# Four engines load the last branch's flag ahead of the experts' stage, and get a branch hint with it

## Chip, cores, metric

The kernel runs on one core of one Trainium2 chip. The metric is the time of one execution in microseconds of device time; the kernel before and the kernel after are compared by their medians over several runs.

## What is computed

The reference is an attention block followed by a mixture of experts. The attention works in chunks of 32 queries, which see 16 keys to the left, 8 to the right and 8 memory keys; its output, with the heads put side by side, is `x` (3072 tokens of 512). Each token goes to the one expert with the largest logit, through two layers, and is weighted by its gate:

```python
for c in range(S // 32):                     # q, k, v: (4, 8, 768, 64)
    a = softmax(scale * q_c @ concat(mem_k, k_ctx).T)
    out[:, :, c_start:c_end] = a @ concat(mem_v, v_ctx)
x = out.transpose(0, 2, 1, 3).reshape(3072, 512)
logits = x @ w_gate                          # 8 experts
e = argmax(logits); gate_w = softmax(logits)[e]
y = gate_w * (maximum(x @ w1[e], 0) @ w2[e]) # w1: (8, 512, 1024), w2: (8, 1024, 512)
```

## The kernel before

There are two programs in the kernel. `ordinary` is the one that these inputs run: it holds for inputs in which no expert gets more than 640 tokens and no sum of exponentials overflows. `general` computes the same for any input. `ordinary` finds out itself whether it was allowed to run, in a flag `good` (L934, a 1x1 tile in SBUF: 1 if its result stands). After it comes `with tc.If(rv == 0)` (L1579), where `rv` is `good` read into a register of each engine (L1137, `values_load`). With these inputs `rv` is 1, so every engine jumps over the code of `general`, which is some hundred instructions on each engine, and the kernel ends.

`ordinary` has two stages.

The **attention stage** (until about 190 us) goes over 32 blocks of 96 queries in a hand-written order (`tc.manual_schedule`): transposes of q and k, scores, exponentials, values, and, a few blocks behind, the routing. Tokens are scattered by expert to `x_dram` in DRAM (L801). Toward its end TensorE already computes up to 256 rows of expert 0 (`do_early`, L1014 writes their `y` on ACT), POOL gathers the rest of expert 0's rows (`xe`, L880), DVE makes sums of weights (`first_sums`, L943), and `count_up` writes `good`. Then the registers are read: `index` (which of 24 code arms each expert takes, TensorE only, L1136) and `rv` (L1137).

The **experts' stage** (from about 190 us to the end) is one `tile_critical` region (L1544) with semaphores of its own. A planner (`op`) has recorded each step with what it reads and writes, and `emit` writes them out with their waits. For each of the 8 experts TensorE enters, by a `Switch` on `index[e]`, one of 24 copies of the same matmuls that differ only in how many tokens they take (L1553). Such a jump goes far, so TensorE gets a hint ahead of it: `switch_hint` names the coming jump and the register that decides it (L1138 for the first expert, L1542 for the others, three steps ahead of an arm's end), and each arm begins with a hint for the jump at its own end. ACT, DVE, POOL and SP run straight on: ACT and DVE take sums out of PSUM and form sums of operands, POOL gathers the next expert's rows (L1293) and sends results to `out` by indirect DMA (L1276, `put`), SP loads weights (L1321). Results go out over five semaphores, `put0` to `put4`. 

On the way into the region every engine waits for all counters of the stage before, so that it is a barrier (L1606: a chain of waits with up to two counters each, and a branch). SP's counter is the last of them, since SP first waits for all work itself. On the way out SP waits until every engine has left the region, and then each engine does the branch at L1579. Behind it, `landed` lets SP wait for the five `put` semaphores, that is, until all output is in DRAM; then all engines meet in a barrier, POOL clears the semaphores, and they meet again (L1606).

## Time and profile before

| | us |
|---|---|
| median of 3 runs | 535.52 (534.76 to 537.1) |
| profiled execution | 532.34 |
| its span, first to last instruction | 530.6 |
| experts' stage, TensorE's first transpose | 190.46 |
| last matmul issued / last store's DMA issued by POOL | 520.8 / 523.9 |
| PE busy | 507.7 (96%) |
| DVE, ACT, POOL busy | 300.0, 245.7, 156.0 |
| granted TensorE clock | 0.994 |

The span's last part is not busy time of any engine: register, branch, wait and semaphore instructions are not counted as busy. They are in the trace all the same, with the engine's name and a q (SPq is SP's sequencer), by line: engine, operation, how many, shortest, median and longest duration in ns, and the start of the first and last in us.

### The profile page before, as it was taken

What the parts mean: (1) busy time and instruction counts of PE and PEld (TensorE: products, weight loads), DVE (VectorE), ACT (ScalarE), POOL (GpSimd) and SP (SyncE); (2) the same over time, 40 slices, a digit from 0 to 9 for tenths busy, and PEclk for the clock granted to TensorE, in tenths of its full rate; (3) what the DMA queues carried; (4) which work ended last, traced back from release to release, by engine and by line L of the source; (5) the groups of instructions that cost most, each with busy time, mean ns of one, the idle gap of its engine ahead of it and who ended that gap; (6) DMA issues with size and microseconds to landing.
All of it is one profiled execution on the core that took longest, in us unless ns stands there. A gap on an engine that the chain in (4) does not pass through costs nothing.

```text
span 530.6 us, 9604 instructions
## 1 busy us (share of the span) xinstructions
PE 507.7 (96%) x3666; PEld 475.7 (90%) x3666; DVE 300.0 (57%) x565; ACT 245.7 (46%) x445; POOL 156.0 (29%) x186
## 2 busy tenths in 40 slices
PE   3999999999999989999999999999999999999992
PEld 3899999999998569999999999977779999999991
DVE  3455656566555246878656557443625767864611
ACT  2466656556632136374553454344216637454311
POOL 2000131323373604354135054121312434412003
PEclk9999999999999999999999999999999999999997
DMA  9999999989982302446406335330505334200002
GB/s 171 154 171 181 182 224 200 224 201 344 303 308 73 88 15 81 172 172 229 176 15 221 96 128 208 102 134 30 195 18 199 139 125 182 81 15 13 1 1 84
DMA packets 81350, 75.02 MB, mean 141 GB/s; under 512 B 39543, under 2 KB 64375, under 8 KB 81281
## 3 DMA queue, kind: packets, MB, share of 16 engines
q1 hardware_dynamic: 71840, 54.60, 41.6%
q0 software_dynamic: 8768, 19.29, 11.0%
q8 instruction: 46, 0.75, 0.6%
q10 hardware_dynamic: 672, 0.18, 0.1%
q14 instruction: 24, 0.19, 0.1%
HBM read 66.13 MB, written 17.50 MB: 158 GB/s over the span
## 4 chain that ended last, share of the span: by engine, by line
PE 83%; issue 9%; DMA 3%; POOL 2%; ACT 1%; DVE 1%; POOLq 0%; ACTq 0%
PE sum_p L511 20%; PE sum_r L511 13%; PE sum_q L511 13%; PE o L511 11%; PE sc L511 8%; PE tqk L516 4%; PE sum_x L516 3%; PE ph L511 3%; PE py L511 3%; PE sum_q L516 2%; PE tx L516 2%; POOL out_dram L1276 2%; DMA xe<-x_dram,rows 1%; DMA x_dram<-xr,dest 1%; DMA kn<-in_k_dram 1%
## 5 line engine op out<-in xcount | busy, mean ns | idle before, releaser
L1276 POOL DMA_INDIRECT out_dram<-y,xe x42 | 51.0, 1214 | 177.1 <-PE sum_q L511 59.9
L1293 POOL DMA_INDIRECT xe<-x_dram,rows x35 | 50.7, 1448 | 49.8 <-PE sum_r L511 29.2
L676 ACT ACTIVATE ex<-sc,cst 128x256 f32<-128x256 f32 x96 | 38.5, 472 | 56.5 <-PE sc L511 56.5
L511 PE MATMUL o<-v,ex 128*96 128x65 f32 x512 | 54.5, 251 | 0.0
L1227 ACT COPY sum_r<-sum_p 128x640 f32<-128x640 f32 x48 | 32.5, 677 | 47.3 <-PE sum_p L511 47.2
L511 PE MATMUL sc<-qT,kT 128*128 128x192 f32 x256 | 50.6, 343 | 1.1 <-ACT qT L627 1.1
L511 PEld LDWEIGHTS o<-v,ex 128*96 128x96 f32 x512 | 49.4, 167 | 0.0
L511 PE MATMUL sum_p<-xsT,w 128*128 128x136 f32 (+6 forms) x256 | 47.6, 329 | 0.5
L511 PE MATMUL sum_r<-t,w 128*128 128x136 f32 (+6 forms) x256 | 45.8, 326 | 0.0
L511 PE MATMUL sum_p<-t,s 128*128 128x136 f32 (+6 forms) x256 | 45.6, 326 | 0.0
L801 POOL DMA_INDIRECT x_dram<-xr,dest x32 | 30.2, 944 | 52.5 <-PE tqk L516 21.3
L511 PE MATMUL sum_q<-t,s 128*128 128x136 f32 (+6 forms) x256 | 45.1, 324 | 0.0
L511 PEld LDWEIGHTS sc<-qT,kT 128*128 128x128 f32 x256 | 43.2, 199 | 1.4 <-issue 1.4
L511 PEld LDWEIGHTS sum_p<-xsT,w 128*128 128x128 f32 x256 | 39.7, 190 | 4.8 <-issue 2.1
L511 PE MATMUL sum_p<-h,w 128*128 128x136 f32 (+6 forms) x256 | 43.8, 324 | 0.0
L511 PEld LDWEIGHTS sum_p<-t,s 128*128 128x128 f32 x256 | 39.7, 190 | 2.6
L511 PEld LDWEIGHTS sum_r<-t,w 128*128 128x128 f32 x256 | 39.6, 190 | 2.6
L511 PEld LDWEIGHTS sum_q<-t,s 128*128 128x128 f32 x256 | 39.8, 190 | 2.3
L511 PEld LDWEIGHTS sum_p<-h,w 128*128 128x128 f32 x256 | 39.5, 190 | 2.3
L1224 DVE TENSOR_TENSOR h<-sum_p,kept 128x640 f32<-128x640 f32 x16 | 13.2, 824 | 48.4 <-ACT sum_r L1227 48.4
L645 DVE COPY kT<-tqk 64x384 f32<-64x384 f32 x62 | 34.3, 554 | 10.4 <-PE tqk L516 9.8
L690 DVE RECIPROCAL inv_all<-o 96x4 f32<-96x4 f32 x64 | 11.4, 179 | 48.0 <-PE o L511 47.7
(154 smaller groups left out, 916.9 us busy)
## 6 DMA issues: line engine op xcount, KB each, us to landing
w<-in_moe_w_dram SPq DMA_DIRECT2D x14, 2048.0 KB, 8.6
kn<-in_k_dram SPq DMA_DIRECT2D x16, 384.0 KB
qn<-in_q_dram SPq DMA_DIRECT2D x16, 384.0 KB
w<-in_moe_w_dram SPq DMA_DIRECT2D x8, 512.0 KB
v<-in_v_dram SPq DMA_DIRECT2D x24, 128.0 KB
v<-in_v_dram SPq DMA_DIRECT2D x24, 112.0 KB
v<-in_v_dram SPq DMA_DIRECT2D x8, 144.0 KB
v<-in_v_dram SPq DMA_DIRECT2D x8, 96.0 KB
```

The lines of the kernel that those rows point to most:

```text
L511: i = nc.tensor.matmul(*args, **more)
L516: i = nc.tensor.transpose(*args)
L645: i = copy(to, of[:, :, 0:PAIRS].rearrange("d a (y z p) -> d a y z p", y=2, z=2))
L676: nc.scalar.activation(ex4[:, :, :, sl], sc4[:, :, :, sl], AF.Exp, bias=mask[:, 3 * x + g : 3 * x + g + 1], scale=D**-0.5)
L690: nc.vector.reciprocal(inv, o[:, :, D])
L801: i = nc.gpsimd.indirect_dma_start(out=x_dram, out_offset=bass.IndirectOffsetOnAxis(ap=dest[:, t : t + 1], axis=0), in_=xr[:, t % NXR].bit ...
L1224: op(eng, one_op(lambda: engines[eng].tensor_tensor(out, a, b, op=how)), reads, writes)
L1227: op("ACT", one_op(lambda: nc.scalar.copy(to, of)), reads, writes)
L1276: return nc.gpsimd.indirect_dma_start(out=out, out_offset=bass.IndirectOffsetOnAxis(ap=which.bitcast(I32), axis=0), in_=y, in_offset=None, ...
L1293: return nc.gpsimd.indirect_dma_start(out=x[:, g].bitcast(I32), out_offset=None, in_=x_dram, in_offset=bass.IndirectOffsetOnAxis(ap=rows[: ...
```

## The change

Two lines are put ahead of the experts' stage. Four engines (POOL, ACT, DVE, SP; not TensorE) compute 1 − rv in a register and run a hint that names the branch of `If` at the kernel's end, which gets a label for that. To compute it they have to have `rv`, so that the load of `good`, which the scheduler puts where a register is first used, stands ahead of the stage on all of them.

```diff
         nc.switch_hint(engines=[nc.tensor], index=[index[e]], n=len(ARMS), label=f"expert{e}")
 
+    for eng in (nc.gpsimd, nc.scalar, nc.vector, nc.sync):
+        tc.mark_branch_hint_location("general", hint=1 - rv, engines=[eng.engine])
     with tc.tile_critical(no_gpsimd_drain=True):
         for e in range(E + 1):
             for s in plan:
@@ -1576,7 +1578,7 @@
             for sem, n in stores:
                 nc.sync.wait_ge(sem, n)
 
-    with tc.If(rv == 0):
+    with tc.If(rv == 0, label="general"):
         landed()
         general(tc, *args)
     landed()
```

In the built program this gives, on each of the four engines, one register operation (`RegisterAlu`) and one `BranchPrefetchHint`. ACT and SP had their load of `good` at that place before; on DVE and POOL it moves there from behind the region. The two moved loads count up the counters of DVE's and POOL's sequencer, which join the counters that every engine waits for on the way into the region: its chain of waits grows by one instruction on each engine, and the counters are paired anew.

## The prediction

> **What bounds the kernel now.** I read the page's head and slices first, then a table of stages, then the sequencer rows of the lines that the change touches (the branch at L1579, the loads of `good` at L1137, the stage's entry and end at L1606 and L1544), and last the DMA view of the tail.

> ```profile
> PE 507.7 (96%) x3666; PEld 475.7 (90%) x3666; DVE 300.0 (57%) x565; ACT 245.7 (46%) x445; POOL 156.0 (29%) x186
> ...
> PE   3999999999999989999999999999999999999992
> ```

> ```profile
> 191.00:470.00 279.00, 278.59 (x1869) 264.04 (x1867) 175.62 (x177) 134.16 (x204) 93.66 (x75) 1.00 0.37 129
> ...
> 525.00:530.60 5.60, 0.00 (x0) 0.00 (x0) 0.00 (x0) 0.00 (x0) 0.00 (x0) 0.50 0.11 37
> ```

> TensorE is busy for 278.59 of 279 us in the experts' stage, so a delay ahead of it is paid in full, and nothing that the four other engines save inside it counts. The last 5.6 us hold no work at all: they are branch, stores, waits and barrier. The rows of the last branch:

> ```profile
> L1579 SPq EVENT_SEMAPHORE  x10: 17/17/17, 526.0 to 526.6; - x10
> L1579 POOLq EVENT_SEMAPHORE  x5: 17/42/43, 526.5 to 526.8; - x5
> L1579 PEldq COMPARE_BRANCH  x1: 3741/3741/3741, 521.3 to 521.3; - x1
> L1579 ACTq COMPARE_BRANCH  x1: 50/50/50, 522.0 to 522.0; - x1
> L1579 DVEq COMPARE_BRANCH  x1: 67/67/67, 522.3 to 522.3; - x1
> L1579 SPq COMPARE_BRANCH  x1: 50/50/50, 522.8 to 522.8; - x1
> L1579 POOLq COMPARE_BRANCH  x1: 53/53/53, 523.3 to 523.3; - x1
> ...
> L1579 ACTq EVENT_SEMAPHORE  x1: 17/17/17, 525.5 to 525.5; - x1
> L1579 DVEq EVENT_SEMAPHORE  x1: 21/21/21, 525.8 to 525.8; - x1
> ```

> Each engine branches over the code of `general`, and its next instruction comes 3.1 to 3.7 us later: ACT 522.0 to 525.5, DVE 522.3 to 525.8, SP 522.8 to 526.0, POOL 523.3 to 526.5; PE has it inside its own row (3.741). In these gaps the DMA records show instruction packets, four of 8 KB between 522.9 and 525.1 and one of 16 KB for PE at 522.7 to 523.7. So the five engines stand still because the branch's target is not loaded.

> **Who ends last.** SP. After its branch it passes ten waits (526.0 to 526.6), stands 0.4 us at a line of instructions that is still being fetched, passes sixteen waits from 527.1 on, among them those for the five queues of output stores (the first of the five, for `put4`, at 527.742), and then goes through barrier and clearing of semaphores to 530.55: 2.81 us from the wait for `put4` to the end. The stores themselves:

> ```profile
> L1276 POOL DMA_INDIRECT out_dram<-y,xe x2: 985/985/985, 522.6 to 523.9; - x2
> ...
> DMA to landing us min/median/max: 3.1/3.4/3.8
> ```

> These are the last two. The last of all starts at 523.895 and lands 3.1 us later, its sixteenth completion at 526.99. SP asks for it at 527.742, so it finds it landed 0.75 us ago. That is the whole slack of the tail: if SP came 3 us earlier, it would wait for this store.

> **The change, part by part.**

> *Two loads leave the tail.* In the order of the built program's instructions, DVE and POOL load `good` after the experts' stage before, and ahead of it after; ACT, SP and PE have always loaded it early.

> ```profile
> L1137 DVEq TENSOR_LOAD <-good x1: 542/542/542, 521.7 to 521.7; - x1
> L1137 POOLq TENSOR_LOAD <-good x1: 504/504/504, 522.8 to 522.8; - x1
> ```

> 0.54 us go from DVE's tail and 0.50 from POOL's, with their branches; SP waits for neither load (its branch stands at 522.780, POOL's load only began at 522.768). Worth nothing by itself. At its new place each load has 2 us or more of cover: DVE ended `s1` at 176.7 and has nothing until 191.6; POOL's next instruction after its gathers is a wait that holds it from 187.4 to 189.6. Without that cover it would be 0.5 us.

> *Four register operations and four hints are added.* The nearest rows are PE's: a hint takes 54 ns at L1138 and 36 to 45 at L1553, a register operation 45. On ACT they stand ahead of the second `y` of the early rows, for which ACT waits 6.2 us anyway; on SP ahead of a wait of 12 us; DVE and POOL as above. On the path: nothing, and at most 0.1 us.

> *The entry to the experts' stage gets longer.* Every engine enters it through a chain of waits on all counters. The two new loads bring two more counters (DVE's and POOL's sequencer). The chain is released by SP's counter (at 189.6, when ACT has ended `y`); before, five waits and the branch follow it, after, seven.

> ```profile
> L1606 PEldq EVENT_SEMAPHORE  x6: 51/51/2005, 187.6 to 190.1; - x6
> L1606 PEldq COMPARE_BRANCH  x1: 197/197/197, 190.2 to 190.2; - x1
> ```

> On PE one such wait follows another at 0.106 us (five of them and the branch fill 189.67 to 190.40). Two more are 0.21 us, ahead of TensorE's first transpose at 190.46: on the path, +0.21. Bounds: 0 if the released engines hide it (they don't: ACT waits for PE there), 0.3 with the hint.

> *Four branches are hinted.* Does a hint work, and does it hold for 340 us? PE's own rows:

> ```profile
> L1553 PEldq COMPARE_BRANCH  x16: 307/319/487, 192.2 to 515.7; - x16
> ...
> L1553 PEldq BRANCH_PREFETCH_HINT  x8: 36/43/45, 192.5 to 470.7; - x8
> ```

> All sixteen hinted branches of PE take 0.31 to 0.49 us, the only unhinted far one 3.74. In the last expert the hint runs at 470.71 and its branch at 515.69, 439 instructions on. PE fetched 16 KB twice between: at 471.4, and at 494.1 as it crossed into the arm's second piece of code; the second can only have been the target, for the branch found it loaded. In the first expert such a fetch (209.43) falls in the stretch where PE goes on without a stall. So a hint is kept, and its target is fetched when the piece with the branch is entered. Nothing in this trace shows a hint on ACT, DVE, POOL or SP, nor one kept over more than one crossing. I take it to work there as on PE.

> Then SP's branch at 522.78 leads on at about 523.1 instead of 525.96, the stop for the next line passes by 524.3, and SP stands at the wait for `put4` from about 524.9. It goes on when the store has landed: 526.99 plus 0.07 (what SP took from the landing of a gather at 187.05 to its next wait at 187.12) is 527.06, against 527.80 for the same step before: **−0.74**. What is late next is the store, and behind it the same 2.75 us. PE's branch is not hinted and ends at 525.0, its part in the barrier at 525.3: under cover. POOL's drain (0.87) moves with POOL to about 524 to 526: under cover.

> *The landing itself.* Four 8 KB fetches (522.9 to 525.1) leave the DMA engines while the last stores go out, and the 16 KB that PE fetches at 525.79 to 527.01 stays. The first two stores of this tail land 1.7 us after POOL has ended them (518.73 to 520.48; 520.02 to 521.72), the last 2.1 (524.88 to 526.99). Bounds: 526.60 by the first, 526.99 by the second. I take the second, since its last completion coincides with the end of PE's fetch, which stays. The other would be another −0.39.

> Sum: +0.21 − 0.74 = **−0.53**. The profiled execution took 532.34 (span 530.6 and 1.74 around it), which gives 531.8; the median of the three runs lies 3.2 above it, so 535.52 − 0.53 = **535.0**.

> [...]

> **The rivals.**

> *The hints change nothing* (the value 1 − rv, which is 0 here, may mean the other side; or an engine other than PE ignores it; or the hint is lost on the way). For it: no row of these engines shows one. Against: PE's sixteen, and the built order, in which `general` follows the branch, so that a jump is the way past it. Then all but the entry's +0.21 is lost: 535.7.

> *The kept hint costs a line in the experts' stage* (the slower side). If these engines give the target the room that their next line needs, the next crossing is a miss: 3.1 us (SP's row) to 3.7 (PE's). The trace shows six 8 KB fetches between 190.9 and 427.4, so ACT or DVE has such crossings, and PE waits for both all through the stage. One miss that PE waits out: 0.21 − 0.74 + 3.1 to 3.7 is +2.6 to +3.2, so 538.1 to 538.7; two make 541 to 542. It decides from one whole miss on. Against it: PE, with a kept hint, ran over its crossings at 209 and 494 without a stall.

> *More than the store's slack is won.* If the end did not hang on the last landing, SP's whole 2.9 us would come off, and 0.5 from POOL: about 532.3. Against it: SP's wait for `put4` is in both orders.

> **How the numbers follow.** The first case 0.78 (own range 534.0 to 536.0: 534.6 with the earlier landing, 535.0 without, and about 0.8 for the runs, half of what a single one of the three shown strays, 534.76 to 537.1, and a little less below), no effect 0.14 (535.7), the lost line 0.06, the large gain 0.02. A measurement of this kernel can tell about 0.5% from no change, 2.7 us. Faster by more 0.02, slower by more 0.06, the rest 0.92. The range takes the two first cases with the runs' spread: 534.0 to 536.5.

> **What would show it right or wrong.** In the profile after: L1579's successor on SP, ACT, DVE and POOL comes within 0.5 us of the branch (if 3 us, the second case); the 8 KB instruction packets between 522.9 and 525.1 are gone; SP's wait for `put4` is a long row that ends with the landing; PE's first transpose comes 0.2 us later than ACT's `y` allows now. A gap of 3 us on ACT or DVE inside the experts' stage, with PE idle beside it, would be the third. A time over 538 or under 533 would make the prediction wrong.

## The result

The kernel after takes 537.49 us (median of 12, 534.5 to 540.29), the kernel before 536.4 (median of its 12 beside it, 534.76 to 538.88; the three shown ahead of the prediction were the first of these). The ratio on record is 1.0012, 95% interval [0.9992, 1.0032] (the two medians alone give 1.0020): not to be told from no change. Forecast were 535.0 and a range of 534.0 to 536.5, so the time lies outside. The profiled execution of after took 538.17 us (span 536.4, clock 0.982), 5.8 us more than that of before. First the page:

```profile
PE   3899999999999989999999999999999999999992
...
PEclk9999999999976999999999999999999999999997
...
q8 instruction: 46, 0.75, 0.6%
...
q14 instruction: 19, 0.16, 0.1%
```

The last of these lines read, before:

```profile
q14 instruction: 24, 0.19, 0.1%
```

The clock's row has a dip in slices 12 and 13 (before, it was 9 there). The table of stages shows the place; the third column from the right is the granted clock (1.00 is full speed), here 0.52 for 14 us of the attention stage and 1.00 after TensorE's first transpose (196.54):

```profile
155.00:169.08 14.08, 14.04 (x65) 12.44 (x64) 5.37 (x32) 2.85 (x7) 5.96 (x12) 0.52 0.21 66
...
196.54:521.00 324.46, 323.90 (x2087) 305.10 (x2088) 194.61 (x196) 150.48 (x227) 99.71 (x80) 1.00 0.32 112
```

That dip ends 10 us ahead of the first instruction that the change adds. One and the same matmul starts 0.5 us earlier than before where before is at 152 us, 5.89 later at 166 and 5.88 later at 186. So all 5.8 us were lost in the dip, where the change isn't, and ahead of the start of ACT's `y` (L1014), 188.80 us before and 194.68 after. Behind it the two profiles differ by 0.06 us. The steps of the prediction are read there, in four stretches: **A**, from that start to TensorE's first transpose; the **stage**, from there to TensorE's last branch at an arm's end; **C**, from the issue of `put4` to its last landing; **D**, from that landing to the end. The **tail** is the last arm's branch to the end, that is 8.2 us to the issue of `put4` (the same in all kernels), C and D.

The entry, TensorE's waits from the one that SP releases (before: six and a branch, 187.6 to 190.2):

```profile
L1608 PEldq EVENT_SEMAPHORE  x8: 51/51/2324, 193.2 to 196.2; - x8
L1608 PEldq COMPARE_BRANCH  x1: 203/203/203, 196.3 to 196.3; - x1
```

Two more, and A goes from 1.66 to 1.86. The last branch, now at L1581, each engine's branch and its next instruction:

```profile
L1581 SPq EVENT_SEMAPHORE  x10: 3/17/680, 529.6 to 531.0; - x10
L1581 POOLq EVENT_SEMAPHORE  x5: 17/43/43, 529.6 to 529.9; - x5
L1581 PEldq COMPARE_BRANCH  x1: 3377/3377/3377, 527.5 to 527.5; - x1
L1581 DVEq COMPARE_BRANCH  x1: 92/92/92, 527.8 to 527.8; - x1
L1581 ACTq COMPARE_BRANCH  x1: 69/69/69, 528.1 to 528.1; - x1
L1581 DVEq EVENT_SEMAPHORE  x1: 21/21/21, 528.5 to 528.5; - x1
L1581 ACTq EVENT_SEMAPHORE  x1: 17/17/17, 528.6 to 528.6; - x1
L1581 POOLq COMPARE_BRANCH  x1: 72/72/72, 529.0 to 529.0; - x1
L1581 SPq COMPARE_BRANCH  x1: 70/70/70, 529.1 to 529.1; - x1
```

DVE 527.8 to 528.5, ACT 528.1 to 528.6, POOL 529.0 to 529.6, SP 529.1 to 529.6: 0.5 to 0.6 us in place of 3.1 to 3.5. The hints work on all four. Before, eight packets of 8 KB lie around the last store, four from 0.97 us ahead of its issue on and four from 2.2 behind it; after, only four are left, from 0.97 ahead to 0.7 behind (the 24 of the page before count a packet of 80 bytes too). So the stretch in which the prediction wanted none is not empty: by their place these are presumably the next lines of code, fetched that much earlier. PE, not hinted, still stands 3.377 us. SP then waits for the store, as forecast (the row of 1669 ns starts at 531.990), and the store lands late:

```profile
L1608 SPq EVENT_SEMAPHORE  x27: 3/28/1669, 531.0 to 536.3; - x27
```
```profile
L1276 POOL DMA_INDIRECT out_dram<-y,xe x1: 983/983/983, 530.0 to 530.0; - x1
...
DMA to landing us min/median/max: 3.6/3.6/3.6
```

C was 3.09 and is 3.61, D was 3.56 and is 2.73. So of the 0.83 us that are won behind the landing, 0.52 went to a store that landed later.

### The profile page after: what moved, and what is told of

Its sections match the earlier page's. It is cut to its first block, busy times and chain, and to the rows that moved or that the text cites. A ratio compares the mean times of both kernels' runs of the same rounds, so it can differ in the third digit from the quotient of the medians.

```text
span 536.4 us, 9620 instructions
## 1 busy us (share of the span) xinstructions
PE 511.5 (95%) x3666; PEld 478.4 (89%) x3666; DVE 299.9 (56%) x565; ACT 245.8 (46%) x445; POOL 155.8 (29%) x186
## 5 line engine op out<-in xcount | busy, mean ns | idle before, releaser
L1276 POOL DMA_INDIRECT out_dram<-y,xe x42 | 50.9, 1211 | 177.5 <-PE sum_q L511 60.1
L511 PE MATMUL sc<-qT,kT 128*128 128x192 f32 x256 | 49.4, 337 | 1.4 <-ACT qT L627 1.4
L511 PEld LDWEIGHTS sc<-qT,kT 128*128 128x128 f32 x256 | 42.0, 195 | 1.9 <-issue 1.4
```

The costliest lines, as they stand in the source:

```text
L511: i = nc.tensor.matmul(*args, **more)
L1276: return nc.gpsimd.indirect_dma_start(out=out, out_offset=bass.IndirectOffsetOnAxis(ap=which.bitcast(I32), axis=0), in_=y, in_offset=None, ...
```

## The experiments

Medians stray by more than the change can bring (the run of the kernel before against itself, below, is off by 1.5 us), so each kernel is read by its stretches. The first eight kernels below were timed 12 or 13 times, each four of them beside 35 runs of the kernel before (median 534.98, then 536.77); the ratio to these and its 95% interval are given. The others ran once each. "Sum" is A, stage and tail: from the start of ACT's `y` to the end.

| profile | A | stage | C | D | tail | sum |
|---|---|---|---|---|---|---|
| before | 1.66 | 325.23 | 3.09 | 3.56 | 14.86 | 341.75 |
| before, second | 1.67 | 325.31 | 4.24 | 2.81 | 15.24 | 342.22 |
| before, third | 1.76 | 325.31 | 3.08 | 3.51 | 14.78 | 341.86 |
| after | 1.86 | 325.29 | 3.61 | 2.73 | 14.54 | 341.69 |
| after, second | 1.97 | **326.94** | 4.04 | 2.73 | 14.96 | 343.87 |
| after, third | 1.86 | **326.93** | 4.07 | 2.73 | 15.00 | 343.79 |
| inverse hint | 1.96 | 325.28 | 4.86 | 2.80 | 15.86 | 343.10 |
| fixed hint | 1.75 | 325.29 | 3.91 | 2.96 | 15.06 | 342.11 |
| SP alone | 1.65 | 325.30 | 3.86 | 2.82 | 14.88 | 341.82 |
| PE alone | 1.77 | 325.21 | 3.45 | 3.52 | 15.17 | 342.15 |
| five hints | 1.87 | **326.94** | 3.37 | 2.73 | 14.30 | 343.11 |
| five, fixed | 1.67 | 325.24 | 2.99 | 2.95 | 14.14 | 341.05 |
| five, fixed, second | 1.77 | 325.30 | 3.04 | 2.96 | 14.19 | 341.26 |
| after, PE late | 1.87 | **326.93** | 2.60 | 6.11 | 16.91 | 345.71 |
| before + 2 waits | 2.02 | 325.30 | 3.98 | 2.80 | 14.98 | 342.30 |
| before + 2, second | 1.93 | **326.91** | 2.87 | 3.82 | 14.89 | 343.72 |
| before + 6 waits | 2.13 | **326.89** | 3.20 | 3.45 | 14.85 | 343.87 |
| before + 6, second | 2.24 | **326.88** | 4.55 | 2.80 | 15.55 | 344.66 |

**The hint's value.** The same loads and waits, the other value:

```diff
-        tc.mark_branch_hint_location("general", hint=1 - rv, engines=[eng.engine])
+        tc.mark_branch_hint_location("general", hint=rv + 0, engines=[eng.engine])
```

> The hint of the four engines takes rv instead of 1 - rv, so that it names the way that is not taken; loads, waits and the number of instructions at the entry stay as after the change. Measured on four stretches of the profile: (A) from the start of ACT's `y` ahead of the experts' stage to PE's first transpose, 1.66 us before, 1.86 after; (B) from PE's last branch at an arm's end to SP's issue of `put4`, 8.2 in both; (C) from that issue to the last landing of `put4`, 3.09 before, 3.62 after; (D) from that landing to the end of the span, 3.56 before, 2.73 after. Theory 1 (the hints work by their value; the entry costs 0.2, the tail gives some 0.3 back, the rest of the difference of the medians is the granted clock): A 1.86, the four branches miss again (2.9 to 3.5 us each), D 3.5, time +0.2 against before, and any larger difference goes with the clock. Theory 2 (the added loads and waits cost some 1 us, by whatever way): +1 against before, as after the change. Theory 3 (a hint fetches the target whatever its value): branches at 0.6, D 2.7.

Measured 536.55 us against 534.98 (ratio 1.0023, [0.9991, 1.0056]).

```profile
L1581 SPq EVENT_SEMAPHORE  x10: 17/17/17, 528.9 to 529.5; - x10
...
L1581 ACTq COMPARE_BRANCH  x1: 54/54/54, 525.0 to 525.0; - x1
...
L1581 SPq COMPARE_BRANCH  x1: 50/50/50, 525.8 to 525.8; - x1
...
L1581 ACTq EVENT_SEMAPHORE  x1: 17/17/17, 528.6 to 528.6; - x1
```

The four engines stand 3.1 to 3.5 us again, so it is the value that does it: 0 names the jump. A is 1.96. D was expected at 3.5 and is 2.80, because the store landed at 4.86, after SP had come. The landing was the surprise of this run, and it stays open: the store's last packet ended at 2.92, 1.94 ahead of it.

**A hint with no register.** The hint's value is fixed, the loads on DVE and POOL go back to the tail, and the entry is that of before:

```diff
-        tc.mark_branch_hint_location("general", hint=1 - rv, engines=[eng.engine])
+        tc.mark_branch_hint_location("general", hint="LikelyTaken", engines=[eng.engine])
```

> The hints of the four engines have a fixed value (likely taken) and no register, so the early loads on DVE, POOL, ACT and their waits are gone, and the entry is that of before. The scheduler puts these hints, which need nothing, at the very start of the program, some 520 us and all of an engine's code ahead of the branch. If a hint is kept until its branch, however many lines of code lie between: A 1.66, branches at 0.6 on four engines, D 2.7, C between 3.1 and 3.6, time -0.3 to -0.7 against before. If only one hint is kept or it is lost at some crossing: all as before, 0.0. PE's own hints are not in question here. Theory 2 (loads and waits cost 1 us): 0 to -0.7, 1 us or more below the kernel after.

Measured 535.36 us (1.0015, [0.9984, 1.0046]). The hints run at 0.71 to 0.77 us of the span, and the branch still finds its target more than 520 us on:

```profile
L1581 ACTq COMPARE_BRANCH  x1: 69/69/69, 524.6 to 524.6; - x1
L1581 DVEq COMPARE_BRANCH  x1: 85/85/85, 524.9 to 524.9; - x1
L1581 ACTq EVENT_SEMAPHORE  x1: 17/17/17, 525.1 to 525.1; - x1
...
L1581 DVEq EVENT_SEMAPHORE  x1: 21/21/21, 525.5 to 525.5; - x1
```

ACT's and DVE's next instructions come 0.5 to 0.6 us behind the branch, SP's at 526.0 behind 525.5 and POOL's at 526.6 behind 526.1. So on these four engines a hint was kept over all of their code here. The tail is 15.06, not 14.0 to 14.5, which the C and D expected add up to: the store again, C 3.91, and D is 2.96 instead of 2.7.

**SP alone.** Of the change's loop only SP is left.

```diff
-    for eng in (nc.gpsimd, nc.scalar, nc.vector, nc.sync):
+    for eng in (nc.sync,):
```

> Only SP gets the hint (with 1 - rv, from the flag that SP loads early in the kernel before as well); DVE, POOL and ACT are as before. Theory 1: A 1.66 (no counter is added to the entry), SP's branch at 0.6, the other three and PE miss (2.9 to 3.7) under cover of the store; SP's wait for `put4` is a long row, D 2.7, and the time is that of the landing: -0.3 (C 3.6) to -0.8 (C 3.1) against before. Rival: ACT's, DVE's or POOL's miss is itself what the end waits for, then D stays at 3.5 and the time at 0.

Measured 535.07 us (1.0005, [0.9977, 1.0034]). SP's branch takes 0.52 us, and then SP stops 3.0 us ahead of the next line of its code (526.85 to 529.88):

```profile
L1581 SPq EVENT_SEMAPHORE  x10: 17/17/17, 526.1 to 526.8; - x10
...
L1581 SPq COMPARE_BRANCH  x1: 70/70/70, 525.6 to 525.6; - x1
```
```profile
L1608 SPq EVENT_SEMAPHORE  x28: 17/28/90, 529.9 to 533.3; - x28
```

Three engines' misses go through the same queue of 8 KB fetches then (q14 of the page); that they delay SP's is likely, and was not tested by itself. SP asks for `put4` at 3.79 us behind its issue, before it was 3.85. Neither reading had this: one engine's hint is worth little while the others miss.

**PE alone.** The change is left out; PE gets a hint behind its last expert, which is tied to its last branch in the built program:

```diff
+            if e == E:
+                LAST.append(nc.tensor.mark_branch_hint_location())
...
+    _bass.BassInstruction(last).branch_hint(LAST[-1], hint="LikelyTaken")
```

> The change is left out and PE alone gets a hint for the last branch (fixed value, placed behind its last expert, some 10 us ahead of the branch). PE's target is then fetched some 8 us earlier instead of beside the last store. Theory 1 with the reading that PE's own fetch of 16 KB holds up the last completion of `put4`: PE's branch takes 0.3 to 0.6 instead of 3.4 to 3.7, the last landing comes with the other fifteen (C 2.75 instead of 3.09), and the time does not move (0.0), because SP's miss still sets the end (D 3.9). Rival: the landing has nothing to do with that fetch: C 3.1 to 3.6. If PE's miss were what the end waits for: D 2.7 and -0.7.

Measured 535.41 us (1.0002, [0.9977, 1.0026]). PE's branch took 1.39 us in place of 3.4 to 3.8, and the time did not move, as expected. C is 3.45, not 2.75, and so in the range named for the rival. PE's next line is now fetched at -0.07 to 0.95 us from the issue of `put4`, beside the data of `put3` (three packets of 4 KB took 0.66 to 0.88 us where most take 0.16; before, two took 0.63 and 0.68), and the four misses of 8 KB are still there; which of them delays the landing isn't shown. The fetch was moved, not taken away.

**Both kernels once more.**

> The changed kernel once more, beside a copy of the kernel before. Stretches as in the first four runs, and the tail from PE's last branch at an arm's end to the end of the span (14.86 before, 14.54 after). Theory 1: A 1.86 to 1.96, experts' stage 325.3, D 2.7 to 2.95; PE's unhinted 16 KB fetch falls on 1.6 to 2.6 us behind the issue of `put4` and the last landing comes about 1 us behind its end (C 3.6 to 3.9), as in the first profile; tail 14.5 to 15.1; so -0.3 to +0.2 in the tail and +0.2 at the entry, a median 0 to 0.4 over that of the copy of before, apart from what happens ahead of ACT's `y`. Theory 2 (the change costs some 1 us of its own): +0.8 to +1.5 over the copy of before, and the profile shows where.

> The kernel before, unchanged, as a control: how far two sets of runs of one and the same kernel stray. Theory 1: the median strays by up to 0.8 from that of the other runs of before of this call, the interval includes 1. In the profile the tail is 14.86 as in the first one as long as the last landing of `put4` comes less than 3.85 us behind its issue (when SP asks for it), since SP's miss is then what the end waits for; A 1.65 to 1.77.

In a second set, on another chip, after took 536.45 us and the copy of before 535.27, against 536.77 for 35 other runs of before: ratios 0.9988 [0.9962, 1.0013] and 0.9974 [0.9945, 1.0003]. The copy strays by 1.5 us from itself, more than the 0.8 expected; medians of a dozen runs can't show what this change does: after lies 1.2 above the copy and 0.3 below the other runs of before. C of the copy is 4.24, so SP came ahead of the landing there too. The profile of after showed something new: the stage takes 326.94 us instead of 325.29. The table of stretches, cut at the edges of the granted clock (last three columns: clock, DMA share, GB/s):

```profile
191.24:194.65 3.41, 1.40 (x11) 1.10 (x11) 0.00 (x0) 1.08 (x2) 0.00 (x0) 1.00 0.01 2
194.66:198.06 3.40, 3.40 (x15) 3.21 (x14) 1.63 (x3) 1.35 (x3) 0.00 (x0) 0.50 0.02 5
198.08:201.48 3.40, 3.40 (x24) 3.17 (x23) 3.37 (x5) 0.80 (x2) 0.00 (x0) 1.00 0.00 0
```

1.1 us behind TensorE's first transpose (193.56) the clock falls to half for 3.41 us, and that is the 1.65 us. In the stretch ahead of it PE is busy for 1.40 of 3.41 us: it stands in the entry.

**All five.** After's four hints and PE's:

> The changed kernel, and PE hinted as well (fixed value, behind its last expert). No engine misses the branch, PE's 16 KB fetches fall at -3.6 and -0.1 us instead of -1.5 and +1.6, the four next lines of 8 KB at -1 to +0.7. Theory 1 with PE's fetch as what holds the last landing: no fetch of any kind in 1.0 to 5.5 us behind the issue of `put4`, so all sixteen landings by 2.8 (3.1 at most); SP waits for it; D 2.7: tail 13.7 to 14.1, that is -0.8 to -1.1 against before; with the entry +0.2: time -0.6 to -0.9. Rival: the last landing strays by itself: C 3.1 to 4.9 here too, tail 14.0 to 15.9.

> All five engines hinted with a fixed value: the four at the start of the program, PE behind its last expert; no early loads, no added counters. DVE and POOL load the flag in the tail again (0.5 each), which moves POOL's part to 0.4 us later. As the run with five hints by the flag, without the entry's cost: A 1.65 to 1.77, all sixteen landings by 2.8 to 3.1, D 2.7 to 2.95, tail 13.7 to 14.2, time -0.7 to -1.1 against before. It is the candidate for the fastest version. Rival: C 3.1 to 4.9.

Measured 536.44 us (0.9992, [0.9965, 1.0019]) and 535.55 (0.9984, [0.9961, 1.0007]). Tails 14.30 and 14.14. The second is as expected. The first is over the 13.7 to 14.1 expected: C is 3.37, which lies in the range that was named for the rival, a landing that strays by itself. With PE's fetch ahead of the store's last data (it ends at 1.04 to 1.33) the landing is 2.99 to 3.37. The version with values by register has the half clock in the stage again, the one with fixed values hasn't.

**PE late.** To see whether PE's fetch holds the landing, it is put behind it:

```diff
+        nc.tensor.wait_ge(sems["put3"], counts["put3"])
         for s, n in counts.items():
             if s not in engines and not s.startswith("put"):
                 nc.gpsimd.wait_ge(sems[s], n)
```

> The changed kernel, and PE waits for the landing of `put3` (about 2.1 us behind the issue of `put4`) ahead of its last branch, so that both of its 16 KB fetches come behind the last store instead of at 1.6 to 3.0. If PE's fetch is what holds the last completion of `put4`: all sixteen landings by 2.85 (C 2.75 to 2.85 instead of 3.6 to 4.0), with the four other engines hinted as after the change. PE's own miss, now 2.2 to 5.6, then is what the barrier at the end waits for, so the tail is no shorter: 14.6 to 15.2. Rival (the last landing strays by itself, or on account of the 8 KB fetches): C 3.1 to 4.9 as before.

```profile
L1276 POOL DMA_INDIRECT out_dram<-y,xe x1: 987/987/987, 529.1 to 529.1; - x1
...
DMA to landing us min/median/max: 2.6/2.6/2.6
```

All sixteen completions are in at 2.60, the lowest of eighteen profiles and below the 2.75 to 2.85 expected. The records of single packets say how it goes in the kernel after. PE's 16 KB fetch is one packet, and lies, counted from the issue of `put4`, at 1.62 to 2.56, 1.58 to 2.99 and 1.94 to 3.02 in the three profiles; the store's last small packet comes directly behind it, at 2.58, 3.01 and 3.04, and the last landing 1.03 us later, at 3.61, 4.04 and 4.07; the fifteen others are in by 2.76. With fixed hints: 1.59 to 2.86, 2.88, 3.91. In all eight of the eighteen profiles in which the store's last four packets of 8 bytes start within 0.05 us of the end of PE's fetch, the landing comes at 3.61 or later; in the ten others at 2.60 to 3.45, but for the 4.86 of the inverse hint. So for the kernel after the cause is shown: the fetch, and not a landing that strays by itself. The start of the fetch alone doesn't decide it (1.94 in the third profile of after, where the packets waited, and 1.90 and 1.96 in two of before, where they didn't); what does is open. The tail came out longer than expected, 16.91 against 14.6 to 15.2: I overlooked that SP's branch waits until PE has left the region (PE's branch stands at 531.3 us here, SP's at 531.4).

**Third profiles.**

> A third profile of the changed kernel. PE's fetch of its next line starts at 1.55 to 1.65 behind the issue of `put4`; last landing 1.0 behind the fetch's end (C 3.6 to 4.1); D 2.73; tail 14.5 to 15.0; A 1.86 to 1.97. A stretch of half clock somewhere in 150 to 200 us of the span moves everything behind it by 2 to 7 us.

> A third profile of the kernel before. SP asks for the landing of `put4` at 3.5 to 3.9 behind its issue; C 3.1 to 4.3; tail 14.86 where the landing is in by then, up to 15.3 where it isn't; A 1.65 to 1.77.

> A second profile of the version with all five engines hinted by a fixed value: A 1.66 to 1.77, PE's fetch of its next line at 0.0 to 1.2, C 2.8 to 3.4, D 2.95, tail 14.0 to 14.6, that is 0.3 to 0.9 less than the kernel before.

All three are within 0.1 of what was expected in A and tail; PE's fetch in after started later than expected (1.94 instead of 1.55 to 1.65), and the landing still came 1.03 behind the last small packet. The single times were 537.03, 535.6 and 533.37. After had 326.93 in the stage once more. That made it four of the six profiles with early loads on DVE and POOL, and none of the eight others.

**What halves the clock.** Within a profile all changes of the granted clock lie whole multiples of 3.413 us apart, so any of them gives the grid: in the first profile of after, stretches of one clock last 139.946, 13.653 and 361.813 us, that is 41, 4 and 106 times 3.413, and in that of before 501.759, 147 times. Laid on it, PE's idle time at the entry (1.90 to 2.01 us in the six, 1.68 to 1.81 in the others) made up a share of one stretch of this grid: at most 0.542 where nothing followed, and 0.557 to 0.588 where the next stretch was halved. That is a theory drawn from the same profiles, so it was put to the test with neither load nor hint, by idle time alone:

```diff
+    gap = tc.alloc_semaphore("gap")
     with tc.tile_critical(no_gpsimd_drain=True):
+        nc.tensor.sem_inc(gap, 1)
+        for _ in range(2):          # and 6
+            nc.tensor.wait_ge(gap, 1)
         for e in range(E + 1):
```

> The kernel before, and PE alone increments a semaphore and waits for it twice ahead of the experts' stage: some 0.2 to 0.35 us more idle time on PE, no load, no hint. The granted clock comes in stretches whose lengths are whole numbers of 3.413 us. Theory of the gate: where PE's idle time at the entry (2.0 to 2.1 us now) lies in one such stretch with a share above 0.55, the next stretch is granted at 0.5 and the stage takes 326.9 instead of 325.3; where it straddles two of them, so that neither share is above 0.53, it doesn't. Rival (the loads, hints or code of the changed kernel): 325.3 in any case.

> As the run with two waits, with six: 0.65 to 0.8 us more idle time (2.35 to 2.6 in all, 0.69 to 0.76 of a stretch), so that the share in one stretch is above 0.55 in more of the positions. Gate: 326.9 with a stretch at 0.5 behind the entry where a share is above 0.55, else 325.3. Rival: 325.3 in any case.

> Once more two waits, for another position of the idle time in the clock's stretches. Gate: 326.9 where a share of a stretch is above 0.55, else 325.3. Rival: 325.3 in any case.

> Once more six waits, for another position of the idle time. Gate: 326.9 where a share of a stretch is above 0.55, else 325.3. Rival: 325.3 in any case.

The waits cost less than expected (idle 1.96 to 2.06 and 2.17 to 2.27). Shares 0.575, 0.636 and 0.666: halved, stage 326.9. Share 0.553, with the remaining 0.051 in the next stretch: not halved, 325.30. By the letter of the expectation ("above 0.55") this last one should have been; the border lies a little higher than it was set. The two runs with two waits, the halved one first and then the other (columns as above):

```profile
192.12:195.53 3.41, 1.45 (x11) 1.05 (x11) 0.00 (x0) 1.04 (x2) 0.00 (x0) 1.00 0.01 5
195.53:198.94 3.41, 3.41 (x16) 3.23 (x15) 1.54 (x3) 1.40 (x3) 0.00 (x0) 0.50 0.02 5
```
```profile
190.90:194.31 3.41, 1.52 (x4) 0.38 (x2) 0.00 (x0) 0.69 (x1) 0.00 (x0) 1.00 0.01 2
194.31:197.73 3.42, 3.25 (x25) 3.17 (x26) 1.52 (x3) 1.76 (x3) 0.00 (x0) 1.00 0.03 7
```

In the second, PE is still idle for 0.17 us behind the edge (3.25 busy of 3.42): the entry lies across it, and less than needed falls on either side. It has the longer idle time of the two (2.06 us against 1.96), so the share of one stretch decides, not the idle time as a whole, and none of the change's loads and hints is needed for it. At this entry, in all eighteen profiles, a share of 0.557 or more (seven) is followed by half clock, and one of 0.553 or less (eleven) is not. It is no rule for the whole program: in the attention stage half clock followed shares of 0.19 to 0.45. The times of the four, 536.54, 540.19, 538.17 and 538.68, hold the dips of the attention stage as well.

## Why the prediction failed

Forecast was 535.52 - 0.53; measured is 537.49. The 2.5 us between are in two places: 0.9 at the start, and 1.6 in the sum (the 0.53 forecast as gain, and the 1.1 by which the two medians of twelve differ).

*The start.* The three runs shown had a median of 535.52, all twelve 536.4. The step that failed is the allowance of "about 0.8 for the runs": two sets of runs of one kernel can be 1.5 us apart. One reason is the half clock of the attention stage, which moves everything behind it: none to five stretches of 3.41 us in the eighteen profiles, up to 8.9 us lost, and the profile that the prediction was worked out from is the only one with none. Another is the start of the program, by which the same matmul stands 2.6 us earlier to 0.6 later than in that profile at 22 us. Which of them set the two sets of runs apart isn't shown. That is 0.9 of the 2.5; by itself it doesn't carry the time out of the range, since 536.4 less 0.53 is 535.9. What sets these first dips is open: PE's idle share ahead of them was 0.19 to 0.45, below what it took at the entry.

*The sum.* By the mean of three profiles each, the sum from ACT's `y` to the end is 341.94 before and 343.12 after, +1.2 instead of -0.53. It fits the medians' difference of 1.1, which alone would show nothing, and in part by luck: after has one profile without and two with the half clock, and the two sets of medians don't agree on how far the kernels are apart.

- *The entry.* Two waits of 0.106 us each: A 1.70 before, 1.90 after, as forecast. But the step "two more are 0.21 us, on the path, +0.21", with 0.3 as the upper bound, is where it failed most. It priced the wait and not what idle time does to the clock behind it: +1.65 us in two of three profiles, so +1.1 by their mean. How often it comes in runs without a profile is not shown: their mean granted clock is 0.9861 with the inverse hint beside 0.9893 for before, but 0.9864 with after beside 0.9865 for before in the second set. Before already has 1.70 us of idle time there, half of one stretch of 3.41, and 1.90 us was enough where it made up 0.557 of one stretch (the third profile of after).
- *The four hints* work as forecast, and together they brought SP to `put4` 1.9 us earlier in the first profile (3.85 to 1.97 behind the issue). From each of the four branches to its engine's next instruction 0.5 to 0.6 us were measured, 3.1 to 3.5 before.
- *The store's landing* was taken at 526.99 with 526.60 as the other bound, that is 3.1 or 2.7 behind the issue. It came at 3.6 to 4.1. The reason given for the choice was PE's fetch, which stays; what was missed is that this fetch can stand ahead of the store's last small packets and hold them, as in all three profiles of after and in one of three of before, whose landing of 4.24 is the late one. The term of -0.74 measured -0.13 (mean tail 14.96 before, 14.83 after).
- *The rivals.* No hint was lost, and no line was missed in the stage; with the half clock out, the stage is 325.2 to 325.3 throughout. The slower side came by a way that no rival named.

A better version: fixed hints for four engines and a hint for PE, which adds nothing to the entry (A 1.67 and 1.77) and takes PE's fetch from the store (C 2.99 and 3.04). Its sum is 341.05 and 341.26, 0.8 less than before, on two profiles. In its runs it can't be told from before.

## What to carry to other kernels

Price a wait on TensorE's path by the whole idle time that it belongs to, not by itself: here, on top of 1.70 us of idle time, 0.2 us more cost 1.65 in the executions in which 0.557 or more of one stretch of 3.413 us was idle. A branch hint took the far branches of four engines from 3.1 to 3.5 us to 0.5 to 0.6, and with a fixed value it needed no register; check what the engine then waits for, and whether an instruction fetch lies beside the transfer that ends the kernel. Where runs stray by more than the change, add up its own stretches in several profiles.
